# Causal masks of the expert scores moved from TensorE to VectorE, in a kernel whose order is planned at build time

## The chip, the cores and the metric

The kernel runs on one core of one Trainium2 chip. A core has five engines that run side by side and wait for each other by semaphores: TensorE (PE, matmuls into PSUM; its weight loads are listed as PEld), VectorE (DVE), ScalarE (ACT), GpSimd (POOL) and SyncE (SP, which here issues the DMAs). The metric is the time of one execution on the device in microseconds (us). Three runs of the kernel before gave 365.78, 366.40 and 366.46 us; the median is 366.4 us.

## The reference, cut to what matters

Three layers follow each other, on 4 batches of 576 tokens and 512 channels:

```python
# 1: attention of 8 heads of 64, twice, and the sum of both
out_up    = repeat(softmax(q4 @ k4.T / 8) @ v4, 4)            # on the means of 4 tokens each
out_local = softmax(where(|i - j| < 4, q @ k.T / 8, -1e9)) @ v
x = out_up + out_local
# 2: four experts of 64, causal attention each; a token uses the best two by its gate logits
logits = x @ w_gate;  w = softmax(two largest logits)
q, k, v = x @ wq[e], x @ wk[e], x @ wv[e]
a = softmax(where(causal, -1e9, q @ k.T / 8))
y = sum over e of w[e] * (a @ v) @ wo[e]
# 3: gated convolution
gate = sigmoid(sum over 5 taps of conv_w[k] * shifted y)
out = (gate * (y @ w_val)) @ w_out
```

`w_val`, `w_out` and `conv_w` come as 64-bit floats; the kernel turns them into 32-bit ones on the chip.

## The kernel before, in words

A batch is worked on in four stages: attention of four pairs of heads (`attention`, `band_scores`, `band_values`, `down_path`), projections to the experts' queries, keys, values and gate logits (`project`, `gates`), the experts' causal attention (`experts`), and the gated convolution with the output product (`tail`, `gated`, `result`). Large products are done as three fp32r matmuls of a high and a low part (`mm3`, lines 1207 to 1210). The stages of neighbouring batches overlap: while the experts of one batch run, the attention of the next one does.

Nothing of that order is written out by hand. Each function adds "pieces" to a `Plan`: a piece is a group of instructions of one engine with an estimated cost, the buffers that it reads and writes, and a due time from the table `DUE`; the table `PICK` says which engine does a piece that two or three engines could do. `Plan.order` (lines 354 to 500) then goes through the pieces as a model of the five engines would run them, always taking the ready piece with the earliest due time, and that gives the order of the instructions in each engine's queue. The model of TensorE has a clock that is at half speed in an interval if the engine was not active enough in the interval before (lines 443 to 447). At run time each engine follows its queue strictly and waits by semaphores.

The places that the change and the prediction touch:

- `expert_scores` (line 1334): scores of 128 queries (T is the number of the block of queries, 0 to 4) against all keys up to their own block, for two experts at once on the two halves of TensorE's rows. Blocks 0 and 1 are one piece, 2 and 3 one each; block 4 (64 queries) goes another way. Lines 1355 to 1360 then add the causal mask inside PSUM: matmuls of an identity with a constant tile `causal` that holds 2^100 above the diagonal. The scores carry a negative sign, so that a masked entry is large and a row's best entry is its minimum.
- `exponentials` (line 1375): VectorE takes the minimum of each row (line 1382, `mmin`), and ScalarE computes exp with that as its bias (line 1390) into the tile `pe` in SBUF. Then weights (`weigh`, line 1438), transposes of `pe` on TensorE (line 1412, for the last block line 1428) and the products with the values (line 1520).
- `chunk` (line 810): conversion of a piece of 64-bit weights. ScalarE makes two 32-bit parts, VectorE a shift (line 856), GpSimd an addition (line 860), and VectorE two operations with two tensors each (lines 864 and 868). There are eight pieces of 512 columns and one of 20.
- `gates` (line 1212): 13 small VectorE operations a batch for the two best experts.
- PSUM has eight banks, shared by kinds of use with a cap each (`PARAMS`: `c_d` is the cap for the large products).

Of the kernel before, what the change touches and what calls it, by code (L numbers as in the profile page):

```python
# [1673 lines left out]
```

## Time and profile before

| | |
|---|---|
| median of 3 runs | 366.4 us |
| the profiled execution, its own time | 365.86 us |
| its span, first to last instruction | 364.1 us |
| mean granted TensorE clock | 0.971 |
| PE busy | 334.5 us, 92% of the span |
| PE weight loads busy | 294.3 us, 81% |
| DVE busy | 303.0 us, 83% |
| ACT busy | 254.9 us, 70% |
| POOL busy | 198.6 us, 55% |

Busy time counts an instruction from its start to its modelled end, and instructions of one engine overlap, so start times are what tells how long a group holds its engine. [...] The stretches below are chosen by what happens in them: the first batch's attention and the weights' conversion (to 54.6 us), its projections and experts (to 109.2 us), the long middle, and the end.

### The profile page before, as it was taken

Reading aid. Unit: us, or ns where it says so; the run is one execution under the profiler, and the core shown is the slowest. Engines: PE = TensorE matmul, PEld = TensorE weight load, DVE = VectorE, ACT = ScalarE, POOL = GpSimd, SP = SyncE. Lnnn points to the kernel's source line nnn. Section 1 sums busy time; section 2 is a strip of 40 time slices with the busy share of each in tenths; the row PEclk is TensorE's granted clock in tenths of the full one; section 3 lists DMA queues with packets and bytes.
Section 4 is the critical chain, followed back from the end, with each engine's and each line's share of the span. In section 5 each row is a group of like instructions: output and inputs, shape, how many; then the busy total and the mean of one; then the engine's idle time right before and its main releaser. Section 6 shows DMA issues by size and latency. Waiting matters only on the chain.

```text
span 364.1 us, 11668 instructions
## 1 busy us (share of the span) xinstructions
PE 334.5 (92%) x4488; PEld 294.3 (81%) x4488; DVE 303.0 (83%) x871; ACT 254.9 (70%) x882; POOL 198.6 (55%) x285
## 2 busy tenths in 40 slices
PE   1478599987999999999999999999999999999996
PEld 1345479965788989989898889998998989897896
DVE  7879989799999858899999897988779548978382
ACT  4887759579898457788787786487757564868251
POOL 5669854646779356398689343267445026534050
PEclk9996879999699999999999999999999999999999
DMA  7978946615312342254560120021100000010022
GB/s 269 210 239 188 247 142 185 164 39 142 54 56 60 113 113 68 82 111 126 142 173 2 34 79 3 0 66 63 38 3 3 4 13 2 29 52 21 0 79 72
DMA packets 26280, 31.72 MB, mean 87 GB/s; under 512 B 2672, under 2 KB 18032, under 8 KB 26224
## 3 DMA queue, kind: packets, MB, share of 16 engines
q1 hardware_dynamic: 26224, 30.97, 31.2%
q8 instruction: 35, 0.57, 0.7%
q14 instruction: 21, 0.17, 0.2%
HBM read 26.24 MB, written 4.72 MB: 85 GB/s over the span
## 4 chain that ended last, share of the span: by engine, by line
PE 71%; DVE 10%; DMA 6%; ACT 5%; POOL 4%; issue 2%; SPq 1%; ACTq 0%; POOLq 0%; DVEq 0%
PE ps L1208 17%; PE ps L1209 15%; PE ps L1210 15%; PE ps L1520 6%; PE ps L1353 5%; PE ps L1412 3%; PE ps L1163 2%; DMA o<-in_wqk_dram 2%; PE ps L1128 2%; PE ps L1097 2%; DMA raw<-in_w_val_dram 2%; DMA qt<-in_qT_dram 2%; POOL wqk_l L808 1%; PE ps L1141 1%; ACT p L1012 1%
## 5 line engine op out<-in xcount | busy, mean ns | idle before, releaser
L1573 POOL TENSOR_TENSOR row<-row,row 128x320 f32<-128x320 f32 (+1 forms) x37 | 29.9, 814 | 44.4 <-ACT row L1561 18.8
L1575 DVE SCALAR_TENSOR_TENSOR row<-ps,cw,row 128x256 f32<-128x256 f32 (+1 forms) x91 | 45.3, 511 | 5.6 <-ACT row L1561 3.0
L1390 ACT ACTIVATE pe<-ps,mmin 128x256 f32<-128x256 f32 (+4 forms) x80 | 41.8, 529 | 7.6 <-DVE mmin L1382 4.6
L1382 DVE TENSOR_REDUCE mmin<-ps 128x1 f32<-128x256 f32 (+4 forms) x80 | 36.3, 475 | 5.0 <-PE ps L1371 2.1
L1208 PE MATMUL ps<-gh,wout_h 128*128 128x256 f32 (+1 forms) x128 | 38.9, 304 | 0.2 <-DVE row L1586 0.2
L1208 PE MATMUL ps<-xh,wqk_h 128*128 128x256 f32 (+1 forms) x128 | 38.3, 300 | 0.3 <-DVE kl L808 0.3
L1209 PE MATMUL ps<-gl,wout_h 128*128 128x256 f32 (+1 forms) x128 | 37.8, 295 | 0.0
L1209 PE MATMUL ps<-xl,wqk_h 128*128 128x256 f32 (+1 forms) x128 | 37.8, 295 | 0.0
L1210 PE MATMUL ps<-xh,wqk_l 128*128 128x256 f32 (+1 forms) x128 | 37.7, 295 | 0.0
L1210 PE MATMUL ps<-gh,wout_l 128*128 128x256 f32 (+1 forms) x128 | 37.7, 295 | 0.0
L1520 PE MATMUL ps<-mp,vE 128*64 128x320 f32 (+4 forms) x224 | 26.9, 373 | 0.3 <-DVE mp L783 0.3
L1012 ACT ACTIVATE p<-ps,mx 128x64 f32<-128x64 f32 x75 | 23.7, 316 | 4.0 <-DVE sm L1035 0.8
L1208 PEld LDWEIGHTS ps<-gh,wout_h 128*128 128x128 f32 x128 | 24.1, 188 | 1.1 <-DVE row L1586 0.5
L1208 PEld LDWEIGHTS ps<-xh,wqk_h 128*128 128x128 f32 x128 | 24.1, 188 | 0.7 <-DVE kl L808 0.5
L808 POOL TENSOR_TENSOR gl<-row,gh 128x256 fp32r<-128x256 f32 (+1 forms) x20 | 16.4, 818 | 14.3 <-ACT gh L791 8.6
L1209 PEld LDWEIGHTS ps<-xl,wqk_h 128*128 128x128 f32 x128 | 24.2, 189 | 0.0
L1210 PEld LDWEIGHTS ps<-xh,wqk_l 128*128 128x128 f32 x128 | 24.1, 188 | 0.0
L1209 PEld LDWEIGHTS ps<-gl,wout_h 128*128 128x128 f32 x128 | 24.1, 188 | 0.0
L1210 PEld LDWEIGHTS ps<-gh,wout_l 128*128 128x128 f32 x128 | 24.1, 188 | 0.0
L1208 PE MATMUL ps<-wvg_h,xh 128*128 128x260 f32 (+1 forms) x80 | 24.0, 300 | 0.1
L783 ACT COPY mp<-ps 128x384 f32<-128x384 f32 (+2 forms) x38 | 17.8, 506 | 8.6 <-PE ps L1412 5.8
L1520 PEld LDWEIGHTS ps<-mp,vE 128*64 128x64 f32 (+1 forms) x224 | 14.2, 137 | 11.7 <-issue 3.5
(221 smaller groups left out, 1206.1 us busy)
## 6 DMA issues: line engine op xcount, KB each, us to landing
qt<-in_qT_dram SPq DMA_DIRECT2D x16, 288.0 KB, 3.9
kt<-in_kT_dram SPq DMA_DIRECT2D x16, 288.0 KB, 4.1
v<-in_vx_dram SPq DMA_DIRECT2D x16, 288.0 KB, 4.9
vw<-in_vx_dram SPq DMA_DIRECT2D x16, 192.0 KB, 4.0
out_dram<-o SPq DMA_DIRECT2D x16, 160.0 KB, 1.8
raw<-in_w_val_dram SPq DMA_DIRECT2D x4, 512.0 KB, 4.9
vw<-in_vx_dram SPq DMA_DIRECT2D x16, 128.0 KB, 4.5
raw<-in_w_out_dram SPq DMA_DIRECT2D x4, 512.0 KB, 3.5
```

Of the source, the lines that this page charges most:

```text
L783: (nc.scalar.copy if eng == "act" else ENG[eng].tensor_copy)(out(), src())
L808: ENG[el].tensor_sub(lo(), src(), hi().bitcast(F32))
L1012: nc.scalar.activation(pv()[:, i], sg(i), AF.Exp, scale=scale, bias=mx.t[:n, i:i + 1], accum_out=sums()[:, i:i + 1])
L1208: nc.tensor.matmul(p, ah, bh, start=first, stop=False)
L1209: nc.tensor.matmul(p, ah, bl, start=False, stop=False)
L1210: nc.tensor.matmul(p, al, bh, start=False, stop=last)
L1353: nc.tensor.matmul(s.t[:, o:o + P * (t + 1)], a.t[r, P * t:P * t + P], z.t[r, :P * (t + 1)], start=(k == 0 and t == T[0]), stop=False)
L1382: nc.vector.tensor_reduce(out=m.t[:, a:a + 1], in_=s.t[:, o:o + n], op=ALU.min, axis=AX.X)
L1390: nc.scalar.activation(pe.t[:, off + c0:off + c1], s.t[:, o:o + c1 - c0], AF.Exp, bias=m.t[:, 0:1], scale=-1.0, accum_out=sums.t[:, a:a + ...
L1520: nc.tensor.matmul(av.t[64 * e:64 * e + 64, z:n], vE.t[:kr, j, 2 * pr + e, :], pT.t[:kr, e, k0:k0 + n - z], start=(j == 0), stop=(j == Tl))
L1573: nc.gpsimd.tensor_add(g.t[:, :nn], g.t[:, :nn], g2.t[:, :nn])
L1575: nc.vector.scalar_tensor_tensor(g.t[:, :nn], x2.t[:, k:k + nn], cw.t[:, m, k:k + 1], g.t[:, :nn], op0=ALU.mult, op1=ALU.add)
```

## The change

- The mask matmuls of query blocks 0 to 3 are gone, and with them the constant `identx`. Instead, `exponentials` uses `tensor_tensor_reduce`: in one VectorE operation it adds a constant tile `later` (0, and 2^100 above the diagonal) to the scores in PSUM, writes them back, and takes the row minimum. It is laid over the last 320 columns at most; a row of 384 or 512 scores first has a plain minimum over the first 64 or 192, which the second operation takes as its start value. Block 4 keeps its mask matmul.
- The conversion of 64-bit weights: one operation with two tensors (line 864) is replaced by a maximum with a constant in place, and the shift works in place too. One 32-bit buffer less is needed.
- In `gates`, five of the operations may go to GpSimd; the copies of the logits may go to ScalarE.
- The planner: TensorE's slow interval is now weighed over four positions of the intervals' edges; several cost formulas are new. `DUE` and `PICK` are new tables, `c_d` is 6 where it was 5, and the softmax's small buffers are 4 where they were 5. The parameter `LATE` is empty, so the new branch that it guards is not built.

```diff
-    "c_d": 5, "c_mo": 3, "c_ms": 3, "c_mt": 6, "c_o": 4, "c_s": 3, "c_t": 4, "c_w": 2, "o_00": 0, "o_01": 1,
+    "c_d": 6, "c_mo": 3, "c_ms": 3, "c_mt": 6, "c_o": 4, "c_s": 3, "c_t": 4, "c_w": 2, "o_00": 0, "o_01": 1,
...
-    0.15, 1.8, 0.55, 5.42, 0.5, 0, 0.35, 7.19, 6.06, 6.94, 3.83, 4.31, 4.54, 4.08, 0, 0.8, 7.39, 0.23,
...
-                    k = int(now / beat)
-                    while len(warm) <= k:
-                        warm.append(active.get(len(warm) - 1, 0.0) >= (0.6 if warm and warm[-1] else 0.97) * beat)
-                    if not warm[k]:
-                        cost *= 2
+                    slow = 0
+                    for off, active, warm in phases:
+                        k = int((now + off) / beat)
+                        while len(warm) <= k:
+                            warm.append(active.get(len(warm) - 1, 0.0) >= (0.6 if warm and warm[-1] else 0.97) * beat)
+                        slow += not warm[k]
+                    cost *= 1 + slow / len(phases)
...
+            nc.gpsimd.memset(later, 0.0)
+            nc.gpsimd.affine_select(out=later[:, LATER - P:], in_=later[:, LATER - P:], compare_op=ALU.is_ge, fill=BIG, base=0,
+                                    pattern=[[-1, P]], channel_multiplier=1)
...
-        @piece("dve", 0.06 + 0.00068 * n, [raw], [a0], kind="port")
+        @piece("dve", 0.066 + 0.00054 * n, [a1], [a1], kind="port")
         def _():
-            v.tensor_single_scalar(part(0), words(1), 3, op=ALU.logical_shift_left)
+            v.tensor_scalar_max(part().bitcast(F32), part().bitcast(F32), LEAST64)
 
-        @piece("pool", gps(n), [a0, f], [f])
+        @piece("dve", 0.066 + 0.00054 * n, [a1], [a1], kind="port")
         def _():
-            nc.gpsimd.tensor_tensor(whole(), part(0), whole(), op=ALU.add)
+            v.tensor_single_scalar(part(), part(), 3, op=ALU.logical_shift_left)
 
-        @piece("dve", vec(n) + 0.09, [a1, f], [f], kind="port")
+        @piece("pool", gps(n), [a1, f], [f])
         def _():
-            v.scalar_tensor_tensor(f.t[:, :n], a1.t[:, :n], TINY64, f.t[:, :n], op0=ALU.is_ge, op1=ALU.mult)
+            nc.gpsimd.tensor_tensor(whole(), part(), whole(), op=ALU.add)
...
+                n = next(count)
+                en = pick("g%d_%d" % (b, n), "dve", "pool")
+                piece(en, time if en == "dve" else 0.34, reads, writes, kind="port")(lambda fn=fn, en=en: fn(ENG[en]))
...
-                                             start=(k == 0 and t == T[0]), stop=False)
-                for t, o in zip(T, at):
-                    for u, d in enumerate((o + P * t, o + P * t + 64)):
-                        for e, s in enumerate(ss):
-                            r = slice(64 * e, 64 * e + 64)
-                            nc.tensor.matmul(s.t[:, d:o + P * t + P], (identb if u == e else identx)[r], causal[r, 0:P - 64 * u],
-                                             start=False, stop=(t == T[-1] and u == 1))
+                                             start=(k == 0 and t == T[0]), stop=(k == 2 and t == T[-1]))
...
-            @piece("dve", vec(c1 - c0), [s], [(m, a)])
-            def _(s=s, o=o, n=c1 - c0, a=a):
-                nc.vector.tensor_reduce(out=m.t[:, a:a + 1], in_=s.t[:, o:o + n], op=ALU.min, axis=AX.X)
+            n, w = c1 - c0, 0 if last else min(LATER, c1 - c0)
+
+            @piece("dve", vec(n, 1 + (n > w > 0)) + TTR * (w > 0), [s] + ([] if last else [late]), [(m, a)] + ([] if last else [(s, "m%d" % e)]))
+            def _(s=s, o=o, n=n, w=w, a=a):
+                least, first, z = m.t[:, a:a + 1], 2 * BIG, slice(o + n - w, o + n)
+                if n > w:
+                    nc.vector.tensor_reduce(out=least, in_=s.t[:, o:o + n - w], op=ALU.min, axis=AX.X)
+                    first = least
+                if w:
+                    nc.vector.tensor_tensor_reduce(out=s.t[:, z], in0=s.t[:, z], in1=later[:, LATER - w:], scale=1.0,
+                                                   scalar=first, op0=ALU.add, op1=ALU.min, accum_out=least)
```

What the tables do to the order is seen in the engines' queues. TensorE, the first batch's scores of query block 2 (384 keys), before: `ps` are PSUM banks, `identb` and `identx` the two halves' identities, `causal` the mask.

```order
L1353 MATMUL ps_65<-kh_124,ql_121 128x384
L1353 MATMUL ps_70<-kh_124,ql_121 128x384
L1359 LDWEIGHTS identb
L1359 MATMUL ps_65<-causal,identb 128x128
L1359 LDWEIGHTS identx
L1359 MATMUL ps_70<-causal,identx 128x128
L1359 LDWEIGHTS identx
L1359 MATMUL ps_65<-causal,identx 128x64
L1359 LDWEIGHTS identb
L1359 MATMUL ps_70<-causal,identb 128x64
L1520 MATMUL ps_64<-mp_144,vE_128 64x256 x2
```

The same place after; the lines of the kernel are counted anew, and line 1358 is the old 1353, line 1139 the old 1141.

```order
L1358 MATMUL ps_65<-kl_125,qh_116 128x384
L1358 MATMUL ps_66<-kl_125,qh_116 128x384
L1358 MATMUL ps_65<-kh_123,ql_118 128x384
L1358 MATMUL ps_66<-kh_123,ql_118 128x384
L1139 MATMUL ps_67<-ident,p_92 128x64
L1139 MATMUL ps_70<-ident,p_92 128x64
```

Between the last score and the next group stood four mask matmuls with a weight load each; now the next group follows at once. Over the whole queue 128 matmuls and 128 weight loads are gone.

VectorE around the row minima of the first batch, before: `mmin` are the minima.

```order
L1180 TENSOR_TENSOR row_104<-ps_63,od_102 128x348
L1382 TENSOR_REDUCE mmin_139<-ps_64 128x1
L1039 RECIPROCAL sm_90<-sm_90 128x3
L1382 TENSOR_REDUCE mmin_140<-ps_67 128x1
L1382 TENSOR_REDUCE mmin_141<-ps_64 128x1
L1050 TENSOR_TENSOR pd_97<-pd_97,sm_90 128x9x48
```

And after, at block 2 of the first batch. The new operation is printed as ISA, in two rows: the pass over the scores, and the read of its result into `mmin`.

```order
L1016 TENSOR_TENSOR p_94<-ps_63,mx_84 128x320
L1001 TENSOR_REDUCE mx_85<-ps_64 128x5
L1385 TENSOR_REDUCE mmin_138<-ps_65 128x1
L1388 ISA ps_65,mmin_138<-ps_65,later,mmin_138 128x320
L1388 ISA mmin_138 128x1
L1385 TENSOR_REDUCE mmin_139<-ps_66 128x1
L1388 ISA ps_66,mmin_139<-ps_66,later,mmin_139 128x320
L1388 ISA mmin_139 128x1
```

One row has become two (128 and 256 scores) or three (384 and 512 scores), and the second of three needs the result of the first.

SyncE's queue from its start, which is the order of the loads, before:

```order
L825 DMA o_165<-in_wvg_dram 128x260
L912 DMA qt_71<-in_qT_dram 128x576
L912 DMA qt_72<-in_qT_dram 128x576
L916 DMA kt_73<-in_kT_dram 128x576
L916 DMA kt_74<-in_kT_dram 128x576
L825 DMA o_166<-in_wvg_dram 128x260
```

And after:

```order
L910 DMA qt_71<-in_qT_dram 128x576
L914 DMA kt_73<-in_kT_dram 128x576
L910 DMA qt_72<-in_qT_dram 128x576
L914 DMA kt_74<-in_kT_dram 128x576
L823 DMA o_163<-in_wvg_dram 128x260
```

The first two pairs' queries and keys (`qt`, `kt`) now go ahead of the first weights.

## Rows read from the trace of the kernel before

**Rows 1.** The page: busy time of each engine, its share, instructions.

```profile
PE 334.5 (92%) x4488; PEld 294.3 (81%) x4488; DVE 303.0 (83%) x871; ACT 254.9 (70%) x882; POOL 198.6 (55%) x285
```

**Rows 2.** Busy time by stretch; columns as named in the first row.

```profile
core 0: us, PE busy (x) PEld busy (x) DVE busy (x) ACT busy (x) POOL busy (x), PEclk, DMA share, GB/s
0.00:27.30 27.30, 12.48 (x222) 8.36 (x222) 21.52 (x53) 19.00 (x71) 16.87 (x44) 1.00 0.87 240
27.30:54.60 27.30, 21.44 (x375) 16.16 (x379) 25.25 (x57) 18.61 (x75) 21.60 (x27) 0.75 0.77 193
54.60:81.90 27.30, 26.02 (x296) 23.00 (x293) 23.71 (x80) 21.02 (x83) 14.30 (x16) 1.00 0.46 129
81.90:109.20 27.30, 23.57 (x365) 19.25 (x360) 26.11 (x80) 25.23 (x92) 19.64 (x26) 0.87 0.35 84
109.20:345.80 236.60, 236.09 (x3149) 213.19 (x3146) 195.73 (x582) 164.01 (x549) 120.94 (x169) 1.00 0.19 54
```

**Rows 3.** Waits of PE in the middle stretch: engine, line, waited for.

```profile
PE ps L1520 <- DVE mp L783: 0.3, 1, 0.3
```

**Rows 4.** Timeline of PE around masks of blocks 2, 3, and 0 with 1.

```profile
197.83 0.23 PE L1359 MATMUL ps<-causal,identx 64*128 64x128 bf16 x1
198.02 0.35 PE L1063 MATMUL ps<-kd,qd 64*64 64x144 f32 x4
...
202.08 0.23 PE L1359 MATMUL ps<-causal,identb 64*128 64x128 bf16 x1
202.18 0.43 PE L1412 MATMUL ps<-ident,pe 64*128 64x64 f32 x7
...
212.91 0.23 PE L1359 MATMUL ps<-causal,identb 64*128 64x128 bf16 x1
213.09 0.38 PE L1141 MATMUL ps<-ident,p 64*128 64x64 f32 x6
```

**Rows 5.** Busy time of the mask line L1359 alone, same columns as Rows 2.

```profile
109.20:345.80 236.60, 5.46 (x100) 2.73 (x100) 1.00 0.19 54
```

**Rows 6.** VectorE by line and shape: count, busy us, mean ns, idle before.

```profile
L1382 DVE TENSOR_REDUCE mmin<-ps 128x1 f32<-128x512 f32 x16 | 10.7, 682 | 0.8 <-ACT rs L1454 0.5 <-PE ps L1359 0.2
L1382 DVE TENSOR_REDUCE mmin<-ps 128x1 f32<-128x384 f32 x16 | 8.3, 549 | 0.2
L1586 DVE SCALAR_TENSOR_TENSOR row<-row,ps 128x320 f32<-128x320 f32 x16 | 7.5, 481 | 0.9 <-PE ps L1210 0.5 <-ACT row L1580 0.2
L864 DVE SCALAR_TENSOR_TENSOR o<-o,o 128x512 f32<-128x512 f32 x8 | 7.2, 895 | 0.0
L1382 DVE TENSOR_REDUCE mmin<-ps 128x1 f32<-128x256 f32 x16 | 6.4, 413 | 1.4 <-PE ps L1359 0.8 <-ACT pe L1390 0.4
L1382 DVE TENSOR_REDUCE mmin<-ps 128x1 f32<-128x128 f32 x16 | 4.4, 282 | 0.3 <-ACT pe L1390 0.2
L856 DVE TENSOR_SCALAR o<-raw 128x512 int32<-128x512 int32 x8 | 3.3, 417 | 0.2
L1290 DVE COPY L<-ps 128x4 f32<-128x4 f32 x16 | 2.5, 155 | 3.7 <-PE ps L1210 3.6
L1386 DVE TENSOR_SCALAR mmin<-mmin 128x1 f32<-128x1 f32 x8 | 1.6, 206 | 0.0
```

**Rows 7.** Timeline of VectorE: two small operations that follow each other.

```profile
163.14 0.17 DVE L1461 RECIPROCAL rs<-rs 128x4 f32<-128x4 f32 x1
163.22 0.17 DVE L1039 RECIPROCAL sm<-sm 128x5 f32<-128x5 f32 x1
```

**Rows 8.** Waits of PE up to 109.2 us, the longest.

```profile
PE ps L1063 <- POOL kd L946: 7.5, 1, 7.5
```

**Rows 9.** Timeline of SyncE's queue from the start.

```profile
0.80 0.39 SPq L825 DMA_DIRECT2D o<-in_wvg_dram  x1
1.24 0.89 SPq L912 DMA_DIRECT2D qt<-in_qT_dram  x2
2.18 0.91 SPq L916 DMA_DIRECT2D kt<-in_kT_dram  x2
```

More of the change, by code (lines that the diff above doesn't have):

```diff
@@ L373, in order @@
         loads = sorted((p for p in self.pieces if p.engine == "sp"), key=lambda p: p.due)[::-1]
-        beat, active, warm = 4096 / 1200, {}, []
+        beat, phases = 4096 / 1200, [(4096 / 1200 * h / 4, {}, []) for h in range(4)]
         port = {"dve": 0.0, "pool": 0.0}
@@ L456, in order @@
                     cost = s + run - now
-                    k = int(s / beat)
-                    while s < now + cost:
-                        z = min(now + cost, (k + 1) * beat)
-                        active[k] = active.get(k, 0.0) + z - s
-                        s, k = z, k + 1
+                    for off, active, _ in phases:
+                        a, k = s, int((s + off) / beat + 1e-9)
+                        while a < now + cost:
+                            z = min(now + cost, (k + 1) * beat - off)
+                            active[k] = active.get(k, 0.0) + z - a
+                            a, k = z, k + 1
                 p.end = now + cost
@@ L512, in vec @@
     return 0.066 * k + 0.00104 * n + 0.127 * chain
+LATER = 320
+TTR = 0.07
 def act(n, sbuf=False):
@@ L519, in gps @@
 def gps(n, k=1):
-    return 0.17 + 0.00185 * n
+    return 0.14 + 0.00215 * n
 def moved(rows, size, queues=16):
@@ L585, in tile_local_attention__then__moe__then__gated_conv @@
         "vd": slots("vd", 1, [P, NC, P]),
-        "mx": slots("mx", 5, [P, NG2]),
-        "sm": slots("sm", 5, [P, NG2]),
+        "mx": slots("mx", 4, [P, NG2]),
+        "sm": slots("sm", 4, [P, NG2]),
         "p": slots("p", 3, [P, 2 * NC * WK2]),
@@ L697, in tile_local_attention__then__moe__then__gated_conv @@
         blanks.append(blank)
-    rests = []
-    for t in pools["pe"]:
-        @piece("pool", 0.23, kind="free")
-        def rest(t=t):
-            nc.gpsimd.memset(t[:, S:], 0.0)
-        rests.append(rest)
     voids = []
@@ L715, in eyeb @@
         nc.vector.tensor_copy(identb, ident)
-    causal = const.tile([P, P], BF16, name="causal")
-    identx = const.tile([P, P], BF16, name="identx")
-    tri = const.tile([P, E, E], F32, name="tri")
+    causal = const.tile([P, 64], BF16, name="causal")
+    later = const.tile([P, LATER], BF16, name="later")
+    tri = const.tile([P, E, E], BF16, name="tri")
     pools["late"] = [None]
@@ L726, in late_constants @@
     def late_constants():
-        @piece("dve", 0.4, [], [late], after=[eye], kind="port")
-        def _():
-            nc.vector.tensor_copy(identx[:, 0:64], ident[:, 64:128])
-            nc.vector.tensor_copy(identx[:, 64:128], ident[:, 0:64])
         @piece("pool", 2.0, [], [late])
@@ L826, in chunk, with part @@
             return f
-        raw, a0, a1 = buf("raw"), buf("o"), buf("o")
+        raw, a1 = buf("raw"), buf("o")
         def words(k, dt=I32):
             return raw.t[:, :2 * n].bitcast(dt).rearrange("p (n t) -> p n t", t=2)[:, :, k]
-        def part(k):
-            return (a0, a1)[k].t[:, :n].bitcast(I32)
+        def part():
+            return a1.t[:, :n].bitcast(I32)
         @piece("sp", 0.5, [], [raw], delay=moved(P, 8 * n), kind="dma")
@@ L846, in _ @@
         def _():
-            nc.scalar.activation(part(1).bitcast(F32), words(1).bitcast(F32), AF.Abs)
+            nc.scalar.activation(part().bitcast(F32), words(1).bitcast(F32), AF.Abs)
         @piece("act", act(n, True) + 0.03, [raw], [f], after=[twos])
@@ L1175, in band_values @@
                 src = xf
-            @piece(en, vec(n) if en == "dve" else gps(n) - 0.1, [src, od], [xf], kind=port(en) if en == "pool" else None)
+            @piece(en, vec(n) if en == "dve" else gps(n), [src, od], [xf], kind=port(en) if en == "pool" else None)
             def _(en=en, src=src, xf=xf, c=c, n=n):
@@ L1210, in mm3, with gates @@
         nc.tensor.matmul(p, al, bh, start=False, stop=last)
-    def gates(L):
+    def gates(b, L):
         ge, gw, gm = buf("ge"), buf("gw"), buf("gm")
@@ L1218, in steps @@
             for time, kind, reads, writes, fn in ops:
-                piece("dve", time, reads, writes, kind=kind)(fn)
+                if kind != "any":
+                    piece("dve", time, reads, writes, kind=kind)(lambda fn=fn: fn(nc.vector))
+                    continue
+                n = next(count)
+                en = pick("g%d_%d" % (b, n), "dve", "pool")
+                piece(en, time if en == "dve" else 0.34, reads, writes, kind="port")(lambda fn=fn, en=en: fn(ENG[en]))
         def le():
@@ L1242, in _ @@
             nc.scalar.activation(gw.t[:, 0], gw.t[:, 0], AF.Exp)
[L1244 to L1248 removed]
+        steps((0.19, "any", [gw], [gw], lambda v: v.tensor_tensor(gw.t[:, 0], gw.t[:, 0], gw.t[:, 1], op=ALU.mult)),
+              (0.19, None, [gw], [gm], lambda v: v.tensor_reduce(out=gm.t, in_=gw.t[:, 0], op=ALU.add, axis=AX.X)),
+              (0.19, "port", [gm], [gm], lambda v: v.scalar_tensor_tensor(gm.t, gm.t, EPS, gm.t, op0=ALU.add, op1=ALU.max)),
+              (0.19, None, [gm], [gm], lambda v: v.reciprocal(gm.t, gm.t)),
+              (0.19, "any", [gw, gm], [gw], lambda v: v.tensor_tensor(gw.t[:, 0], gw.t[:, 0], by_token(gm.t), op=ALU.mult)))
         pw, ew = bank("d"), buf("ew")
@@ L1286, in project, with _ @@
                  lambda p=p, r=r: p.t[:r, 0:256].rearrange("p (e d) -> p e d", d=64), [p, late], [(y["vE"], t)])
-            @piece("dve", 0.1, [p, late], [(L, t)])
-            def _(p=p, r=r, t=t):
-                nc.vector.tensor_copy(L.t[:r, t, :], p.t[:r, 256:260])
-        y["w"] = gates(L)
+            el = pick("lo_%d%d" % (b, t), "dve", "act")
+            @piece(el, 0.1 if el == "dve" else act(4), [p, late], [(L, t)])
+            def _(p=p, r=r, t=t, el=el):
+                (nc.scalar.copy if el == "act" else nc.vector.tensor_copy)(L.t[:r, t, :], p.t[:r, 256:260])
+        y["w"] = gates(b, L)
         for sp, (n0, nn) in enumerate(SPLIT):
@@ L1343, in expert_scores @@
             at = [sum(P * (u + 1) for u in T[:k]) for k in range(len(T))]
-            @piece("pe", sum(3 * f32r(P * (t + 1)) + 0.15 for t in T), [(qh, (mine,)), (ql, (mine,)), (kh, half), (kl, half)], ss,
-                   kind="row", size=20 * len(T))
+            @piece("pe", sum(3 * f32r(P * (t + 1)) for t in T), [(qh, (mine,)), (ql, (mine,)), (kh, half), (kl, half)], ss,
+                   kind="row", size=12 * len(T))
             def _():
@@ L1387, in exponentials @@
         for a, (s, o, c0, c1) in enumerate(sp):
-            @piece("act", act(c1 - c0) + 0.187, [s, m], [(pe, off if len(sp) == 1 else c0), (sums, "%d%d%d" % (T, e, a))])
+            @piece("act", act(c1 - c0) + 0.187, [s if last else (s, "m%d" % e), m], [(pe, off if len(sp) == 1 else c0), (sums, "%d%d%d" % (T, e, a))])
             def _(s=s, o=o, c0=c0, c1=c1, a=a):
@@ L1421, in keys_on_rows @@
         pe, pts, nf = pes[0], [bank("mt"), bank("mt")], T + 1
-        @piece("pe", 0.067 * nf, [pe], pts + [(pT, "%dt" % T)], after=rests, kind="row", size=4 * nf)
+        @piece("pe", 0.067 * nf, [pe], pts + [(pT, "%dt" % T)], kind="row", size=4 * nf)
         def _():
@@ L1427, in _ @@
                     r, j = slice(64 * u, 64 * u + 64), T - k
-                    nc.tensor.transpose(pt.t[:, 64 * k:64 * k + 64], pe.t[r, j * P:(j + 1) * P], ident[r, r])
+                    kr = min(P, S - j * P)
+                    nc.tensor.transpose(pt.t[:kr, 64 * k:64 * k + 64], pe.t[r, j * P:j * P + kr], ident[r, r])
         def place(u):
@@ L1503, in experts @@
             for pr in range(2):
-                pT, vE, av = buf("mp%d" % g), y["vE"], bank("mo")
+                pT, vE, av, rows = buf("mp%d" % g), y["vE"], bank("mo"), (b, g) not in LATE
+                rs, es = None if rows else buf("rs"), buf("es") if g else None
                 for Ts in ((0, 1),) if g == 0 else ((2,), (3,), (4,)):
                     pes = [buf("pe") for _ in range(2 if Ts[0] < NTOK - 1 else 1)]
-                    sums = buf("es" if Ts[-1] == NTOK - 1 else "rs")
+                    sums = es if Ts[-1] == NTOK - 1 else rs or buf("rs")
                     for T, e, sp in expert_scores(y, pr, Ts):
-                        exponentials(T, e, sp, sums, pes[e], P if Ts == (0, 1) and T else 0, Ts.index(T))
-                    weigh(b, y["w"], pr, Ts, sums, pes)
+                        exponentials(T, e, sp, sums, pes[e], P if Ts == (0, 1) and T else 0, Ts.index(T) if rows else T % 2)
+                    if rows:
+                        weigh(b, y["w"], pr, Ts, sums, pes)
                     keys_on_rows(b, pr, Ts, pes, pT, base, w, P * (Ts[-1] - T0))
@@ L1521, in _ @@
                                              pT.t[:kr, e, k0:k0 + n - z], start=(j == 0), stop=(j == Tl))
-                ah, al = y["ah"][g], y["al"][g]
-                split("a%d%d%d" % (b, g, pr), lambda av=av, n=n: av.t[:, :n], n, lambda ah=ah, pr=pr, n=n: ah.t[:, pr, HALO:HALO + n],
-                      lambda al=al, pr=pr, n=n: al.t[:, pr, HALO:HALO + n], av, (ah, str(pr)), (al, str(pr)))
+                ah, al, r = y["ah"][g], y["al"][g], av
+                if not rows:
+                    r = factors(b, y["w"], g, pr, T0, n, rs, es)
+                    @piece("dve", vec(n), [av, r], [r])
+                    def _(av=av, r=r, n=n):
+                        nc.vector.tensor_tensor(r.t[:, :n], av.t[:, :n], r.t[:, :n], op=ALU.mult)
+                split("a%d%d%d" % (b, g, pr), lambda r=r, n=n: r.t[:, :n], n, lambda ah=ah, pr=pr, n=n: ah.t[:, pr, HALO:HALO + n],
+                      lambda al=al, pr=pr, n=n: al.t[:, pr, HALO:HALO + n], r, (ah, str(pr)), (al, str(pr)))
                 if g == 0:
```

53 lines of the change are left out of this document (24 added, 29 removed), and 425 rows, old and new, of the table DUE.

## The prediction

> **What bounds the kernel now.** I read the busy times first [rows 1]: PE is busy for 92% of the span, DVE for 83%, and both are averages over unlike stages. So I cut the span into stretches [rows 2]. From 109.2 to 345.8 us PE is busy for 236.09 of 236.60 us at the full clock, and its listed waits there come to 0.3 us [rows 3]: that stretch is as long as PE's queue, and DVE (195.73 us busy) has 40.9 us to spare. Before it, it is otherwise. Up to 27.3 us PE is busy for 12.48 us, behind the loads (DMA share 0.87) and DVE (21.52). From 27.3 to 54.6 us DVE is busy for 25.25 of 27.30 us, PE for 21.44 at a clock of 0.75. From 54.6 to 81.9 PE is nearly full (26.02). From 81.9 to 109.2, the first batch's experts, DVE is full again (26.11) and PE is at 23.57 and 0.87. The reader is to see that an instruction taken from PE is worth its time after 109.2 us, and that one put on DVE costs something before it.
>
> **Masks off PE.** The durations of the mask matmuls overlap, so start times count. From the first mask to the first matmul behind the group: block 2, 198.02 - 197.83 = 0.19 us; block 3, 202.18 - 202.08 = 0.10; blocks 0 and 1 together, 213.09 - 212.91 = 0.18 [rows 4]. That is 0.47 us for one batch and one pair of experts, and there are 8 of these: 3.8 us. As a check, the weight loads of 100 of the 128 masks take 2.73 us in the middle stretch [rows 5], or 3.5 us for all; their busy time of 5.46 us (7.0 for all) holds the matmuls' tails, which overlap the next group. Bounds: 0, if PE must wait for something else in these places, and 7.0 us. I take 3.8, since it is what start times show; 100/128 of it, 3.0 us, lies in the full stretch, and the rest in the experts of batch 0, where DVE decides together with PE.
>
> **Masks onto DVE.** Today 64 minima cost 16 x (0.282 + 0.413 + 0.549 + 0.682) = 30.8 us [rows 6]. After: the new pass over 128 or 256 scores, 16 x (0.282 + 0.413), and over 320, 32 x 0.481 (the row of line 1586, which also reads one tensor from PSUM and one from SBUF, as the pass does), together 26.5 us. The minima over the first 64 and 192 columns: by the slope of the four rows, (682 - 282)/384 = 1.04 ns per column, they are 0.215 and 0.348 us, 16 of each, 9.0 us. The 64 reads of the result: no such row on DVE; I take 0.155 us, the copy of four columns, 9.9 us (bounds 0.07 us, its start-to-start share, and 0.206). For 32 passes that need the minimum just before them, 206 - 155 = 0.05 us each, 1.6 us. Sum 47.0, or 16.2 us more in durations. But a DVE instruction starts before the end of the one ahead: 163.22 against 163.14 + 0.17 [rows 7], 0.09 us, and 96 instructions more take back 96 x 0.09 = 8.6. Net 7.6 us more of DVE. No row has DVE write a wide result into PSUM: at the price of the nearest rows it is free; were it to halve the rate, see the slower rival.
>
> [...]
>
> **DVE relieved.** Conversion: eight operations with two tensors, 8 x 0.895 = 7.2 us, and eight shifts, 3.3 us, go; sixteen in-place operations with a constant come, which I price as the shift, 16 x 0.417 = 6.7 us. Gain 3.8 us (between 0, if they meet GpSimd on their way, and 7). The copies of the logits: 15 of 20 go to ScalarE, 2.3 us. Of the gates, 12 small operations go to GpSimd, some 4 us, and `identx` costs 0.6 us less. Together 10.7 us against 7.6 us: DVE's total stays where it is, within 3 us, which the other choices of engine (more softmaxes in one pass on DVE, fewer of their normalizations there) do not change by more. POOL is at 55% and ACT at 70%, and neither is what PE waits for in the long stretch.
>
> **What comes earlier.** PE's first matmul waits 7.5 us for the first pairs' pooled keys [rows 8]. Two DMAs of queries and two of keys are issued from 1.24 and 2.18 us on, 0.45 us each, behind a load of weights at 0.80 [rows 9]. Without it the last of the four is issued at 0.80 + 3 x 0.45 = 2.15 instead of 2.63: 0.5 us (bounds 0, if DVE's or GpSimd's part decides, and 0.9). Three of the eight large conversions lie in the DVE-bound stretch up to 54.6 us and give 3/8 of 3.8 = 1.4 us, of which I take 1.0, as DVE is 92% busy there. In the experts of batch 0 the new passes cost a quarter of 7.6 us, 1.9, and five conversions, gates and logits give 2.4 + 1.0 + 0.6 = 4.0; I take nothing for the difference of 2.1, since where the conversions fall is the new order's choice. The rest of the new order I take as equal, since its rows can't be timed. The new `c_d` frees no bank, it only allows another split of the eight.
>
> **The sum.** Against the profiled execution's own 365.86 us: -3.8 (masks) - 0.5 (first loads) - 1.0 (conversion) + 0 (DVE's exchange) = 360.6 us. The median of the runs shown is 366.4, 0.5 us above that execution, so I predict 361.1 us, 1.4% faster. What a measurement of this kernel can tell from no change is about 0.2%, 0.7 us.
>
> **Rivals.** *The new order also takes out PE's early stalls and slow stretches.* For it: up to 109.2 us PE is idle for 25.7 us (109.2 less 12.48, 21.44, 26.02 and 23.57) and its clock stands at 0.75 and 0.87 in two of the four stretches [rows 2], and this is what the planner's new weighing is about. Against: DVE and the loads bound much of it, and they carry as much as before. At 0.75 of the clock half the stretch ran at half speed, at 0.87 a quarter of it; a return to the full clock would save 1.9 us of the ten full microseconds before 54.6 and 3.1 us in the experts, 5.0 in all. Time: 356.1 us. The same in the other direction, a new slow stretch of that size, would end at 366.1 us.
>
> *The new wait takes the saving.* A row of 512 scores takes DVE 0.348 + 0.481 + 0.155 + 0.05 - 2 x 0.09 = 0.85 us instead of 0.68, one of 384 0.72 instead of 0.55, one of 128 or 256 0.155 - 0.09 = 0.07 more, and exp, the transposes and the products follow in line. For one batch and pair that is 4 x 0.17 + 4 x 0.07 = 0.96 us, 7.7 us in all. For it: in the experts of batch 0 DVE is full and PE is not [rows 2]. Against: in the long stretch PE has other work in between, and waits 0.3 us. If two thirds reach PE, 5.1 us, the time is 366.2 us: no change.
>
> *Slower: the new pass runs at half the rate.* It covers 16 x (128 + 256) + 32 x 320 = 16384 columns; at twice 1.04 ns that is 17 us more on DVE, first in the experts of batch 0, where DVE has 1.2 us free of 27.3: a quarter, 4.3 us, is paid in full. Of the other 12.8 us, in a stretch where DVE is 83% busy, I count a third as paid, 4.3 us. Time: 361.1 + 8.6 = 369.7 us. It decides from a duration of some 0.65 us for 320 columns (0.48 by the rows). For it: no row shows a wide PSUM write on DVE. Against: of reading PSUM and SBUF together there is a row, at the full rate.
>
> [...]
>
> **How the numbers follow.** The forecast, 358.5 to 364.5 us, has a chance of 0.45; the order that also takes out stalls 0.26; the saving lost to waits or to a new slow stretch 0.13; the slow pass 0.16. Faster by over 0.2% (below 365.7): all of the first two and a third of the third, 0.75. Within 0.2%: half of the third, 0.07. Slower: 0.18. The range reaches from the second case's 356 to between the third and the fourth: 355.5 to 368.5 us.
>
> **What would show it.** Line 1358 followed by other groups without a gap, PE's rows fewer by 128; the new pass at 0.28, 0.41 and 0.48 us for 128, 256 and 320 columns and its read below 0.2 us; DVE's busy time within 5 us of 303 plus overlaps; the long PE-bound stretch still at 99% or more, and shorter; the first matmul at about 7.0 us. The prediction is wrong if the pass takes over 0.65 us, if PE shows waits for exp (line 1390) of more than 3 us after the first batch, or if PE's clock falls in stretches where it was full.

## The result and the profile after

The changed kernel takes 360.66 us (median of four runs, 359.92 to 361.21) against 366.14 for the kernel before, also of four: a ratio of 0.985, 95% interval 0.983 to 0.987, so 1.5% or 5.5 us faster. 361.1 was predicted. The profiled execution has a span of 358.8 us, 5.3 less than before.

The page's busy times, answering to [rows 1]:

```profile
PE 328.0 (91%) x4360; PEld 288.2 (80%) x4360; DVE 293.8 (82%) x933; ACT 257.6 (72%) x870; POOL 198.3 (55%) x289
```

The same stretches as [rows 2], with the same columns:

```profile
0.00:27.30 27.30, 10.26 (x148) 6.65 (x148) 18.70 (x52) 16.53 (x54) 19.15 (x44) 0.91 0.93 240
27.30:54.60 27.30, 21.83 (x451) 16.18 (x450) 22.20 (x61) 20.79 (x71) 20.36 (x26) 0.84 0.84 203
54.60:81.90 27.30, 27.30 (x408) 24.42 (x408) 24.88 (x86) 24.85 (x95) 13.80 (x18) 1.00 0.48 134
81.90:109.20 27.30, 23.02 (x389) 18.65 (x386) 27.13 (x99) 25.73 (x97) 21.58 (x29) 1.00 0.58 144
109.20:345.80 236.60, 235.83 (x2914) 212.86 (x2913) 194.23 (x625) 165.79 (x548) 120.67 (x172) 1.00 0.16 46
```

And what is left behind the long stretch, before and after:

```profile
345.80:364.10 18.30, 14.95 (x102) 14.30 (x101) 10.68 (x23) 7.02 (x16) 5.25 (x7) 0.98 0.22 75
345.80:358.80 13.00, 9.79 (x68) 9.50 (x66) 6.61 (x16) 3.94 (x10) 2.77 (x4) 1.00 0.26 91
```

PE has 128 matmuls fewer and is still full after 109.2 us. From there to its end it is busy for 236.09 + 14.95 = 251.04 us before and 235.83 + 9.79 = 245.62 after: 5.4 us less, about the whole gain. That says how much work was left at 109.2 us, not yet why. DVE is nearly free of idle time in the experts of batch 0 (27.13 of 27.30 us, 26.11 before). The clock changed in both directions before 109 us: 0.91 where it was 1.00, 0.84 where it was 0.75, 1.00 where it was 0.87. In twenty equal slices of each of the stretches with 0.75 and 0.87 the clock of before stands at 0.50 or at 1.00 of full speed, but for six slices between such (0.56 to 0.57 and 0.93 to 0.94): 0.75 is about half the time at half speed.

The minimum on DVE by line and shape, answering to [rows 6]: line 1385 is the first part (and the unmasked block 4), line 1388 the new pass and the read of its result.

```profile
L1388 DVE CUSTOM_DVE_ANT_0 ps<-ps,later,mmin 128x320 f32<-128x320 f32 x32 | 17.9, 559 | 1.1
L1388 DVE DVE_READ_ACCUMULATOR2_ANT mmin<- 128x1 f32 x64 | 9.0, 140 | 0.0
L1388 DVE CUSTOM_DVE_ANT_0 ps<-ps,later 128x256 f32<-128x256 f32 x16 | 6.6, 433 | 0.8 <-ACT pe L1397 0.8
L1385 DVE TENSOR_REDUCE mmin<-ps 128x1 f32<-128x192 f32 x16 | 5.5, 345 | 0.0
L1388 DVE CUSTOM_DVE_ANT_0 ps<-ps,later 128x128 f32<-128x128 f32 x16 | 4.3, 311 | 2.6 <-PE ps L1358 2.0 <-ACT mp L781 0.6
L854 DVE TENSOR_SCALAR o<-o 128x512 f32<-128x512 f32 x8 | 4.1, 517 | 1.8 <-ACT o L845 1.8
L858 DVE TENSOR_SCALAR o<-o 128x512 int32<-128x512 int32 x8 | 3.5, 439 | 0.0
L1385 DVE TENSOR_REDUCE mmin<-ps 128x1 f32<-128x64 f32 x16 | 3.5, 218 | 1.1 <-PE ps L1358 1.0
```

The pass takes 0.311, 0.433 and 0.559 us where the prediction had 0.28, 0.41 and 0.48; the slow rival's mark was 0.65. From 128 to 256 columns that is 0.95 ns a column, where the minima of before took 1.04. Its read takes 0.140 us. Lines 854 and 858 are the conversion's two in-place operations; the last row is the minimum over 64 columns.

Start times of two rows of 384 scores on VectorE (columns: start, duration, engine, line):

```profile
184.85 0.21 DVE L1385 TENSOR_REDUCE mmin<-ps 128x1 f32<-128x64 f32 x1
185.09 0.56 DVE L1388 CUSTOM_DVE_ANT_0 ps<-ps,later,mmin 128x320 f32<-128x320 f32 x1
185.57 0.14 DVE L1388 DVE_READ_ACCUMULATOR2_ANT mmin<- 128x1 f32 x1
185.57 0.22 DVE L1385 TENSOR_REDUCE mmin<-ps 128x1 f32<-128x64 f32 x1
```

A row takes 185.57 - 184.85 = 0.72 us, as predicted. PE's longest waits over the whole program, answering to [rows 3, 8]; line 1061 was 1063, its first matmul:

```profile
PE ps L1061 <- DVE kd L944: 7.2, 1, 7.2
PE ps L1139 <- DVE sm L1033: 6.5, 1, 6.5
PE ps L1120 <- DVE sm L1033: 4.6, 4, 2.7
```

The first matmul's wait fell from 7.5 to 7.2 us, but not that of the group behind it. PE's start before (first two lines) and after:

```profile
7.54 2.36 PE L1063 MATMUL ps<-kd,qd 64*64 64x144 f32 x24 [7.54 <-POOL kd L946]
12.37 0.48 PE L1122 MATMUL ps<-band,identb 64*64 64x320 bf16 x4 [2.46 <-ACT sm L1033]
7.22 0.75 PE L1061 MATMUL ps<-kd,qd 64*64 64x144 f32 x4 [7.22 <-DVE kd L944]
8.33 1.70 PE L1061 MATMUL ps<-kd,qd 64*64 64x144 f32 x20 [0.36 <-POOL kd L944]
12.72 0.48 PE L1120 MATMUL ps<-band,identb 64*64 64x320 bf16 x4 [2.68 <-DVE sm L1033]
```

Only four of the 24 matmuls come earlier; the other 20 wait for GpSimd until 8.33 us, and the next group starts at 12.72 us where it started at 12.37. The three long waits lie before 109 us; between 109.2 and 345.8 us PE's listed waits come to 0.7 us.

### The profile page after: what moved, and what is told of

Same layout as the page of the kernel before. It is cut to its first block, busy times and chain, and to the rows that moved or that the text cites. A ratio compares the mean times of both kernels' runs of the same rounds, so it can differ in the third digit from the quotient of the medians.

```text
span 358.8 us, 11453 instructions
## 1 busy us (share of the span) xinstructions
PE 328.0 (91%) x4360; PEld 288.2 (80%) x4360; DVE 293.8 (82%) x933; ACT 257.6 (72%) x870; POOL 198.3 (55%) x289
## 4 chain that ended last, share of the span: by engine, by line
PE 64%; DVE 14%; DMA 8%; POOL 5%; ACT 4%; issue 3%; SPq 1%; ACTq 0%; POOLq 0%; DVEq 0%
PE ps L1206 16%; PE ps L1207 14%; PE ps L1208 14%; PE ps L1530 6%; DVE row L1592 4%; PE ps L1358 4%; DMA v<-in_vx_dram 3%; PE ps L1419 3%; DMA raw<-in_w_val_dram 2%; PE ps L1126 2%; DVE ps L1388 1%; PE ps L1061 1%; DMA o<-in_wvg_dram 1%; DMA raw<-in_w_out_dram 1%; PE ps L1161 1%
## 5 line engine op out<-in xcount | busy, mean ns | idle before, releaser
L1397 ACT ACTIVATE pe<-ps,mmin 128x128 f32<-128x128 f32 (+4 forms) x80 | 41.8, 526 | 15.2 <-DVE mmin L1388 9.1
L1590 POOL TENSOR_TENSOR row<-row,row 128x320 f32<-128x320 f32 (+1 forms) x35 | 29.1, 834 | 33.4 <-ACT row L1578 14.0
L1206 PE MATMUL ps<-xh,wqk_h 128*128 128x256 f32 (+1 forms) x128 | 39.2, 306 | 0.0
L781 ACT COPY mp<-ps 128x384 f32<-128x384 f32 (+2 forms) x43 | 20.4, 500 | 8.6 <-PE ps L1419 6.4
L1498 POOL TENSOR_SCALAR pe<-pe,rs,gw 128x384 f32<-128x384 f32 (+3 forms) x29 | 19.1, 663 | 13.6 <-DVE rs L1469 4.3
L1206 PE MATMUL ps<-wvg_h,xh 128*128 128x260 f32 (+1 forms) x80 | 23.2, 291 | 0.0
L1207 PE MATMUL ps<-wvg_l,xh 128*128 128x260 f32 (+1 forms) x80 | 22.9, 286 | 0.0
L1208 PE MATMUL ps<-wvg_h,xl 128*128 128x260 f32 (+1 forms) x80 | 22.8, 285 | 0.0
```

The costliest lines, as they stand in the source:

```text
L781: (nc.scalar.copy if eng == "act" else ENG[eng].tensor_copy)(out(), src())
L1206: nc.tensor.matmul(p, ah, bh, start=first, stop=False)
L1207: nc.tensor.matmul(p, ah, bl, start=False, stop=False)
L1208: nc.tensor.matmul(p, al, bh, start=False, stop=last)
L1397: nc.scalar.activation(pe.t[:, off + c0:off + c1], s.t[:, o:o + c1 - c0], AF.Exp, bias=m.t[:, 0:1], scale=-1.0, accum_out=sums.t[:, a:a + ...
L1498: ENG[en].tensor_scalar(v, v, x, y, op0=ALU.mult, op1=ALU.mult)
```

## The experiments

Times are medians. They are compared by their ratio to the kernel before on the same chip (medians there 366.3 to 367.3); the kernel after has 0.9849, and 0.9834 when it ran again with the last group. Two ratios whose intervals overlap are told apart, where they are, by their traces.

**Masks left out of the kernel before.**

```
-    nc.tensor.matmul(s.t[:, d:o + P * t + P], (identb if u == e else identx)[r], causal[r, 0:P - 64 * u], ...)
```

> The kernel before, order and all else unchanged, with the mask matmuls of blocks 0 to 3 (line 1359) left out, so that the scores of those blocks are not masked. It measures what these matmuls cost PE in the old order. The prediction's step (start times, 0.47 us for a batch and pair, 3.8 us in all) expects 366.1 - 3.8 = 362.3 us. The rival reads the profile after otherwise: PE's time from the first matmul to the end fell by 5.0 us, of which about 4 lie before 109 us, where its waits and slow stretches changed; then the masks are worth what is left, 1 to 2 us, and this run ends at 364.1 to 365.1. A second rival has PE waiting for exp instead: 366.

Measured: 365.01 us, ratio 0.998 (0.994 to 1.001). In the ratio the masks are worth 0.9 us, not resolved from none; the 3.8 us of the prediction lie outside the interval. The trace is sharper, since every group of scores stands at the same place in both orders. Here a block 2 without masks, and the matmul behind it:

```profile
195.53 0.42 PE L1353 MATMUL ps<-kh,qh 64*128 64x384 f32 x2
195.79 0.34 PE L1353 MATMUL ps<-kl,qh 64*128 64x384 f32 x2
195.96 0.34 PE L1353 MATMUL ps<-kh,ql 64*128 64x384 f32 x2
196.23 0.97 PE L1063 MATMUL ps<-kd,qd 64*64 64x144 f32 x24
```

The same group in the kernel before, whose first mask and follower are in [rows 4]:

```profile
197.21 0.42 PE L1353 MATMUL ps<-kh,qh 64*128 64x384 f32 x2
197.47 0.34 PE L1353 MATMUL ps<-kl,qh 64*128 64x384 f32 x2
197.65 0.34 PE L1353 MATMUL ps<-kh,ql 64*128 64x384 f32 x2
```

From the first score to the follower it took 198.02 - 197.21 = 0.81 us with masks and 196.23 - 195.53 = 0.70 without: 0.11 saved, not 0.19. The last pair of scores now steps 0.27 us to the next kind of matmul, where it stepped 0.18 to the first mask. So 0.09 us of the masks' step was the change of group, and that stays. Over the 24 groups, one with a wait left out, the difference sums to 2.7 us, of which 2.2 in the groups whose masks come after 109.2 us (100 of the 128).

**Masks back on PE in the kernel after**, with one plain minimum over the row.

```
+    for t, o in zip(T, at): ... nc.tensor.matmul(s.t[:, d:o + P * t + P], ..., causal[r, 0:P - 64 * u], ...)
-    tensor_reduce over n - w; tensor_tensor_reduce over w
+    nc.vector.tensor_reduce(out=least, in_=s.t[:, o:o + n], op=ALU.min, axis=AX.X)
```

> The kernel after, in its own order, with the masks of blocks 0 to 3 put back on PE as 16-matmul groups and one minimum over the whole row on DVE in place of the two-step one. It undoes the change's first half alone. By the prediction's sum PE pays 3.8 us again and DVE is relieved of 7.6 us net, of which a quarter (1.9 us, the experts of batch 0) is worth time at most: 360.7 + 3.8 - 0 to 1.9 = 362.6 to 364.5 us. If the gain came from the new order, masks are worth 1 to 2 us: 360.7 to 362.7 us.

Measured: 362.29 us, ratio 0.989 (0.984 to 0.994), 1.6 us more than after. That is inside the second theory's range and 0.3 us below the first's: masks moved are worth some 1.6 of the 5.5 us (2.1 by the second ratio of after), but the intervals overlap, so the times alone do not resolve it. The next run, beside this one on the same chip, has the same single minimum and no masks: 360.23 us, so the masks alone cost PE 2.1 us here. That difference is clear of the noise (the means differ by 2.0 us, with a 95% interval of 0.7 to 3.4). From PE's first matmul to its last this trace has 2.3 us more than that of after, near the 2.7, but only 0.7 more than the second trace of after: the two traces of after differ by 1.6 us. At the same places, the 22 of 24 groups of scores that have no wait in this trace nor in that of after take 2.9 us longer with masks.

**No masks at all in the kernel after** (the plain minimum, masks left out everywhere).

```
-    tensor_reduce over n - w; tensor_tensor_reduce over w
+    nc.vector.tensor_reduce(out=least, in_=s.t[:, o:o + n], op=ALU.min, axis=AX.X)
```

> The kernel after, in its own order, with one plain minimum over the row in place of the two-step one, so that the scores of blocks 0 to 3 are not masked anywhere. It measures what the masks cost on DVE now. By the prediction's sum, nothing (DVE has room after 109 us, and what the new passes cost before it is paid back elsewhere): 360.7 us; if the quarter of 7.6 us in the experts of batch 0 is paid, 1.9 us less: 358.8. By the rival that the new wait takes the saving (two thirds of 7.7 us reach PE) it would be 5.1 us less: 355.6.

Measured: 360.23 us, ratio 0.984 (0.980 to 0.988). DVE's busy time fell from 293.8 to 287.4 us, and the time by 0.4, not resolved from none. The 358.8 of the second theory lies at the interval's lower edge. The rival that the new wait takes the saving, 355.6, falls. In the experts of batch 0 the clock of this shorter execution (358.5 us) is as low as it was before:

```profile
81.90:109.20 27.30, 24.60 (x388) 20.61 (x384) 25.73 (x83) 25.39 (x97) 20.96 (x30) 0.87 0.55 145
```

**One pass over the whole row.**

```
-    if n > w: tensor_reduce(... s.t[:, o:o + n - w] ...)
+    tensor_tensor_reduce over all n columns, in1=later[:, 512 - n:]
```

> The kernel after, in its own order, with the row's masked minimum in one pass over 384 or 512 scores instead of a minimum over the first 64 or 192 and a pass over 320; the output is the same. By the rows after, 128 columns take 311 ns and 256 take 433, so by that slope 384 take 555 and 512 take 677, against 218 + 559 and 345 + 559: 0.22 us less for each of 32 rows, less 0.09 of overlap lost with each instruction, 4.3 us of DVE. If DVE bounds the experts of batch 0, a quarter of it is worth time: 359.6 us. If DVE's work is hidden everywhere: 360.7 us.

Measured: 360.69 us, ratio 0.984 (0.979 to 0.988): no difference seen. DVE's busy time fell by 3.8 us, to 290.0. But the 359.6 of the first theory, a ratio of 0.982, lies inside the interval, so this run does not decide between the two. It shows the pass over more columns, with a constant as its start value:

```profile
L1388 DVE CUSTOM_DVE_ANT_0 ps<-ps,later 128x384 f32<-128x384 f32 x16 | 8.7, 569 | 1.2 <-PE ps L1358 1.1
```

**The pass over 320 done twice.**

```
-    if w: tensor_tensor_reduce(...)
+    for _ in range(2 if n > w > 0 else w > 0): tensor_tensor_reduce(...)
```

> The kernel after, in its own order, with the new pass over 320 scores done twice in the 32 rows that have it (the same output, since what is masked stays masked). It adds 32 x (0.559 + 0.140 - 2 x 0.09) = 16.6 us to DVE, as much as the pass at half the rate would have. By the slower rival's price (a quarter in full in the experts of batch 0, a third of the rest) 8.3 us: 369.0 us. If only the experts of batch 0 are bound by DVE: 364.8 us. If the wait for the minimum reaches PE nowhere: 361 us.

Measured: 379.01 us, ratio 1.036 (1.031 to 1.041): 18.3 us more than after. No theory had that. A row on VectorE:

```profile
169.13 0.56 DVE L1388 CUSTOM_DVE_ANT_0 ps<-ps,later,mmin 128x320 f32<-128x320 f32 x1
169.61 0.14 DVE L1388 DVE_READ_ACCUMULATOR2_ANT mmin<- 128x1 f32 x1
169.78 0.56 DVE L1388 CUSTOM_DVE_ANT_0 ps<-ps,later,mmin 128x320 f32<-128x320 f32 x1
```

The second pass starts 169.78 - 169.13 = 0.65 us after the first, not 0.52. It needs the value just read, and starts 169.78 - 169.61 = 0.17 us after the read, where a minimum that does not need it starts together with the read (185.57). That is 32 x 0.65 = 20.8 us of DVE in all. The long stretch, and what PE waits for from 109.2 us on:

```profile
109.20:345.80 236.60, 224.98 (x2771) 200.01 (x2769) 200.07 (x653) 158.50 (x532) 117.81 (x166) 1.00 0.16 45
```

```profile
PE ps L1206 <- ACT pe L1397: 3.5, 5, 1.4
PE ps L1206 <- DVE mp L781: 1.7, 2, 1.4
PE ps L1258 <- DVE row L1603: 1.2, 1, 1.2
```

DVE still has 36.5 of 236.6 us to spare there, and yet PE lost 235.83 - 224.98 = 10.9 us. By these waits it was not DVE's total that was late, but each row's minimum, then exp (line 1397, which waited 16.3 us for line 1388 where it had waited 9.1), then what PE's fixed queue has next.

**The same, with the planner told.**

```
-    vec(n, 1 + (n > w > 0)) + TTR * (w > 0)
+    vec(n, 1 + (n > w > 0)) + TTR * (w > 0) + 0.52 * (n > w > 0)
```

> The run with the new pass over 320 scores done twice (379.0 us, 18.3 us slower than after), with one more edit: the planner is told of the 0.52 us that each second pass takes, so the order is made anew around it. If those 18 us were lost because the order was made for shorter passes, and DVE's spare time can hide them once PE is given other work in between, a good part comes back: 364 to 370 us. If the wait for the minimum is bound to reach PE: 379 us.

Measured: 393.4 us, ratio 1.072 (1.068 to 1.077): worse still. Neither theory had that. The planner was told of 0.52 us where the step is 0.65. A likely reason is that the due times were made for another list of costs, so that a new order drawn from them is worse than the old one with late instructions; no run shows it by itself.

**Conversion with a two-tensor operation.**

```
-    v.tensor_scalar_max(part()..., part()..., LEAST64)
+    v.scalar_tensor_tensor(part()..., part()..., LEAST64, part()..., op0=ALU.max, op1=ALU.max)
```

> The kernel after, in its own order, with the first of the conversion's two in-place operations on DVE made one with two tensors, like the one that the change took out (895 ns in place of 517 for 512 columns): the same output, and 8 x 0.38 = 3.0 us more DVE. By the prediction (3/8 of the conversion's gain counts before 54.6 us, and it is the DVE-bound part) 3/8 x 3.0 = 1.1 us more: 361.8 us. If DVE's work there is hidden: 360.7 us.

Measured: 362.18 us, ratio 0.988 (0.984 to 0.992), 1.2 to 1.7 us more than after by its two ratios, whose intervals overlap this one's: a loss of the expected size, not resolved from none. The operation took 0.812 us on average, so 8 x (0.812 - 0.517) = 2.4 us of DVE were added. The clock from 27.3 to 54.6 us is down to 0.71, where the two traces of after have 0.84 and 0.81.

```profile
27.30:54.60 27.30, 22.02 (x438) 16.39 (x437) 19.71 (x54) 19.26 (x68) 19.29 (x23) 0.71 0.80 180
```

**Logits and gates back on DVE.**

```
-    (nc.scalar.copy if el == "act" else nc.vector.tensor_copy)(L.t...)     fn(ENG[en])
+    nc.vector.tensor_copy(L.t...)                                           fn(nc.vector)
```

> The kernel after, in its own order, with the 15 copies of logits given to ScalarE and the 12 small gate operations given to GpSimd back on DVE; same output. By the prediction they are 2.3 and some 4 us of DVE, of which about a quarter (0.6 + 1.0 us) falls in the experts of batch 0 and is worth time: 362.3 us. If DVE's work there is hidden, or the wait is another: 360.7 us.

Measured: 363.14 us, ratio 0.990 (0.987 to 0.992), against 361.11 of the kernel after beside it: 2.0 us. The edit adds DVE time in all four batches, and the loss is in the later ones. The long stretch, and PE's longest waits in it:

```profile
109.20:345.80 236.60, 233.77 (x2891) 210.07 (x2890) 195.17 (x643) 162.44 (x530) 115.84 (x158) 1.00 0.16 46
```

```profile
PE ps L1161 <- DVE L L1295: 1.0, 1, 1.0
PE ps L1161 <- ACT pe L1397: 0.8, 1, 0.8
PE ps L1206 <- DVE ge L1237: 0.8, 1, 0.8
```

PE is 2.1 us less busy there (235.83 after), and lines 1295 and 1237 are the moved operations. Small DVE work that comes a little later stops PE, beside 41 us of DVE's idle time. This is the price in an order that was made for ScalarE and GpSimd. The kernel before had these operations on DVE in an order of its own, and PE waited 0.3 us in this stretch [rows 3]; so the 2.0 us are not what moving them gained.

**Old tables on the new code, and new tables on the old code.**

```
-DUE, PICK of the kernel     +DUE, PICK of the other kernel, piece by piece; c_d and the planner's positions with them
```

> The code after with the order of before: due times, choices of engine and c_d = 5 carried over piece by piece, and one position of the clock's intervals in the planner; the copies of the logits and the gates stay on DVE. The old numbers were made for the old code, so this is the new code in an order that is not its own. By the prediction's sum, in which the order is worth nothing and the first loads 0.5 us: 361.2 us. By the rival that the order takes out PE's early stalls and slow stretches, which the profile after bears out before 109 us (4 us): 364 to 365 us.

> The code before with the order of after: due times, choices of engine, c_d = 6 and the four positions of the clock's intervals carried over; masks on PE and the old conversion. By the prediction's sum only the first loads come earlier: 366.1 - 0.5 = 365.6 us. By the rival that the order is worth 4 us: 362 us. Either may be spoilt, since the order was made for other durations; then it is slower than 366.1 us, and says that order and code go together.

Measured: 400.55 us, ratio 1.094 (1.089 to 1.099), and 378.77 us, ratio 1.034 (1.030 to 1.039). Both are spoilt. What the new order is worth by itself can't be had in this way; neither kernel's tables fit the other's list of pieces and costs.

**One position of the clock's intervals.**

```
-    phases = ..., [(... * h / 4, {}, []) for h in range(4)]
+    phases = ..., [(0.0, {}, [])]
```

> The kernel after with the planner's model of the clock at one position of its intervals instead of four, all tables as they are; the order comes out otherwise from the first transposes on. By the prediction's sum the order of one position is as good as that of four: 360.7 us. If the weighing of four positions holds stalls and slow stretches down, or the tables fit only the order they were made with: 364 us or more, with waits or a lower clock before 109 us.

Measured: 378.93 us, ratio 1.032 (1.029 to 1.035). The long stretch, where the clock is full:

```profile
109.20:345.80 236.60, 231.26 (x2811) 203.06 (x2809) 190.15 (x608) 160.44 (x540) 120.32 (x168) 1.00 0.17 47
```

Weight loads fell from 212.86 to 203.06 us in it, and PE's busy time from 235.83 to 231.26: less work was done there at the same clock, so the order is worse. This doesn't show four positions to be better than one, only that these tables do worse with one.

**The kernel after, once more.**

> The kernel after, unchanged, on the chip of the other three runs, to compare them with. 360.7 us, if this chip is like the first.

Measured: 361.11 us, ratio 0.983 (0.980 to 0.987). Its clock in the second and fourth stretch was not that of the first trace:

```profile
27.30:54.60 27.30, 21.85 (x441) 16.02 (x441) 20.35 (x55) 18.88 (x66) 17.97 (x24) 0.81 0.74 171
81.90:109.20 27.30, 23.89 (x443) 19.64 (x442) 27.13 (x101) 25.80 (x95) 21.57 (x31) 0.94 0.62 153
```

The same program had 0.84 and 1.00 there. So a difference of 0.06 between two traces says nothing of two kernels.

## Why the prediction was right, step by step

The time was right to 0.4 us, and so was the main mechanism: PE's queue bounds the time after 109 us (busy for 235.83 of 236.60 us there), so a matmul taken from it is time saved. That the sum came so close is in part luck, since its terms are off and cancel. By place, the sum has 3.0 us of masks in the full stretch and 2.3 us before it (0.8 of masks, 1.5 of the rest). Measured, 5.4 us less of PE's work is left at 109.2 us. Of these, 2.2 us are masks, and 3.2 us are other work that PE now gets done earlier.

- **Masks off PE, -3.8 us: mis-sized.** The step from the first mask to the follower holds the change of group, 0.09 us in the block 2 shown, which stays with the last score. Measured at the same places, 2.7 us; by the runs 0.9 us (old order, not resolved from none) and 2.1 us (new order, resolved) reach the end.
- **Masks onto DVE, 0 of the sum: held as far as the runs resolve it.** Without them the time is 0.4 us shorter, within the noise. The row's 0.72 us was right, by another split: the read takes no time from start to start (it and the next minimum both start at 185.57), and the pass with a start value is 0.08 us longer than taken. The overlap that the sum took back held too: 185.57 against 185.09 + 0.56, 0.08 us.
- **DVE relieved, taken as spent on the new passes: this step failed.** Both were netted because their totals were alike. They were not: DVE's busy time fell by 9.2 us, outside the 5 us allowed. The new passes cost 6.4 us (by the run without them), so some 15.6 us left DVE, where 10.7 were counted. The conversion gave only 10.5 - 4.1 - 3.5 = 2.9 of its 3.8 us; what was left out is the other choices of engine, which the prediction held to 3 us. DVE has 7 normalizations `pd<-pd,sm` before and none after, 14 and 8 of `p<-p,sm`, 24 and 17 of `pe<-pe,rs,gw`, some 15 us less together, while the pass `p<-ps,mx` of its softmaxes grew from 17 to 24. Nor has time on DVE a single price: putting logits and gates back costs 2.0 us, while taking the masks' passes away brings no resolved gain. It depends on whether something that PE's queue has next stands behind the operation.
- **Conversion, -1.0: borne out in size, not resolved.** 1.2 to 1.7 us by its run, for 2.4 us of DVE.
- **First loads, -0.5: this step failed.** The first matmul comes 0.3 us earlier (7.54 to 7.22), but only four do; the rest wait for GpSimd, and the next group starts 0.35 us later than before. In the other trace of the old order, without masks, the first matmul waits 8.1 us, so traces differ here by 0.6 us, more than the term, and no gain is shown.
- **The clock: one of the prediction's own signs of being wrong came.** Up to 27.3 us it fell from 1.00 to 0.91, and the second trace of after has 0.94; PE is busy for 10.26 of 27.30 us there, and no run shows what it costs.

The measured parts do not add up to a proof: masks 2.1 us and conversion 1.2 to 1.7 are prices of undoing one thing in an order that was made with it, and the 2.0 us of logits and gates is not a gain over the kernel before at all. Where the rest of the 5.5 us comes from stays open.

Of the rivals, the slow pass fell by its duration (0.559 us, its mark 0.65). Had it come, its price would likely have been far above the 8.6 us given: the doubled pass cost 18.3 us for its 20.8, where 8.6 had been counted for 17. The rival of stalls and slow stretches fell by its size, 356.1 us, but not as a part of the cause: 3.2 us of PE's work do move ahead of 109.2 us. The clock's mean does not tell how, since the run without masks had 0.87 in the experts of batch 0, as before the change, and was no slower than after. How much of the 5.5 us the new order gives, and how much the relief of DVE, stays open; no run could separate the order from the code that it was made for.

## What to carry to other kernels

In this kernel, whose queues are fixed at build time, an engine's idle share was not a reserve: 20.8 us more on an engine with 42 us to spare in its long stretch cost 18.3, and 6.4 us less gave 0.4, within the noise. Price an added operation by what waits behind it, not by its engine's share, and do not expect its removal to give back what its addition would cost. Whether a new order would make more of the removal, no run shows. Price a removed group of matmuls by the same place with and without it: here 0.09 us of the last step was the change of group, which did not go away. And when a sum comes out right, see whether its terms do: here 15.6 us left VectorE where 10.7 had been counted, and the time was right all the same.

## What was not expected of the hardware

The read of the accumulated minimum, 0.140 us by duration, shifts nothing: the next instruction starts at the same time (185.57). A pass over 320 columns with its start value from memory takes 0.559 us. With a constant as start value 256 columns take 0.433 and, in the run of one pass, 384 take 0.569, so that 320 would take 0.50: an estimate, by which the start value from memory, or the wait for it, costs some 0.06 us.

Means can mislead: the in-place maximum over 512 columns took 0.517 us on average, where the shift of before took 0.417 [rows 6]. But it is one of the eight that took 1.197 us (it started at 20.90, while GpSimd was in an instruction from 20.55 to 21.81), and the median of the line is the shift's time (columns: shortest, median and longest in ns, first and last start):

```profile
L854 DVE TENSOR_SCALAR o<-o x9: 160/416/1197, 10.9 to 103.4; 128x512 f32<-128x512 f32 x8, 128x20 f32<-128x20 f32 x1
```
